# An order planner for attention and two gated layers on one core: measured lengths, a smaller early margin, eight drawn orders

## The chip, the cores and the metric

The kernel runs on one core of one Trainium2 chip. The metric is the device time of one execution in microseconds; the median of several runs counts. A program on one core has no other core to wait for.

## What is computed

The reference, cut to what matters (2 batches, 8 heads, 768 positions, heads of 64; blocks of 32 keys, a window of 16):

```python
k_sum = k.reshape(B, H, nb, block, D).max(axis=3)
v_sum = v.reshape(B, H, nb, block, D).mean(axis=3)
scores_l = where(|i - j| < window, scale * q @ k.T, -1e9)      # near keys
scores_s = scale * q @ k_sum.T + log(block)                    # one key per block
a = softmax(concatenate([scores_l, scores_s]))
x = a @ concatenate([v, v_sum])                                # [1536, 512]
h = sigmoid(x @ w_gate) * (x @ w_val)                          # 512 -> 1536
y = h @ w_out                                                  # 1536 -> 512
h2 = maximum(maximum(y @ w1, y @ w2), y @ w3)                  # 512 -> 768
out = h2 @ w_out2                                              # 768 -> 512
```

## The kernel before

The work is written as tasks. A task has an engine, a length in microseconds that stands in the code, a due time, the tasks that it needs, and the buffers that it takes and uses. `Plan.order` (line 123) is a list scheduler: it keeps a clock for each engine, takes at each step the task that can start first on its engine (among those within a small slack the one with the earliest due time), and so writes one order. `Plan.latest` walks that order backwards and gives each task the latest start that would not move the end; `Plan.refined` makes an order, takes these starts as new due times, orders again (`REFINE` is 2, so three orders in all), and keeps the one with the earliest end. The kernel is then emitted in that order. On the chip every engine runs its own instructions strictly in it, and what a task needs from another engine is waited for by semaphores. So a wrong length or landing time in the planner does no harm to the result, but an engine then stands at an instruction whose input is not there while later ones could run.

Transfers into the chip are issued by SyncE (SP) in one queue. The planner lets a landing follow the place in the queue, each transfer taking its length times `SLOW`, and adds a margin `LATE` of 2.0 us behind every transfer that ends after `CALM`, 4 us.

The attention is cut into 16 units: batch, pair of heads (4), half of the sequence. A unit's steps are: block maxima of the keys (`kmax`, line 802, VectorE); block sums of the values on TensorE (`vsum`, line 809), evacuated (814), folded (`vfold`, 817) and copied out (829); scores on TensorE, near keys (`k` or `kx` with `q` or `qx`) and block keys `ks` (both line 901); row maxima with the mask on VectorE (908); exponentials on ScalarE (914); a reciprocal on VectorE (919, 920); scaling on ScalarE (928) or VectorE (923); transposes on TensorE (933), evacuated by ScalarE (939, tile `at`); the product with the values (`v` or `vx`, line 946); and its split into two fp32r parts (465, 468). A unit whose number is even uses `v`, an odd one `vx`; in the first batch an odd head pair uses `kx` and `vnx`. Every fp32 weight block arrives as `raw`, is put into fp32 form on VectorE (535, 540, 544, tile `c` or `cx`) and split into two parts `w` on ScalarE and VectorE (465, 468).

The gated layer's matmuls for the first batch (line 1044, `x` with `w`, three for each of four chunks of the contraction, so 12 for one accumulator) begin once four units of the first batch are transposed; four PSUM banks `m` hold their accumulators, and each is freed by a sigmoid on ScalarE (1061) or a product on VectorE (1068). Exponential and sigmoid need different activation tables, so each change between them is an `ACT_TABLE_LOAD`. While the attention's first units run, TensorE has little to do; there, up to `FIRST` + 5 us of the planner's clock, the planner puts filler matmuls on a zero tile `idle` (line 1781) into its gaps, to keep its clock up. They are instructions like all others and have to run before what stands behind them.

Numbers at the ends of tile names, as in `e_432`, count buffers in the order in which they are taken; the first four units of the first batch are `e_149/150`, `e_236/237`, `e_333/334` and `e_432/433` in the kernel before and `e_149/150`, `e_202/203`, `e_326/327` and `e_474/475` in the changed one.

Of the kernel before, what the change touches and what calls it, by code (L numbers as in the profile page):

```python
# [14 lines left out]
ALU = mybir.AluOpType  # L15
# [6 lines left out]
FIRST = 28.0  # L22
# [18 lines left out]
REFINE = 2  # L41
SECOND_ORDER = (1, 2, 0)
# [5 lines left out]
SLOW = 1.12  # L48
BANKS_H, BANKS_W, BANKS_T = 9, 10, 5
# [30 lines left out]
class Plan:  # L80
# [7 lines left out]
    CALM, LATE = 4.0, 2.0  # L88
# [34 lines left out]
    def order(self):  # L123
# [18 lines left out]
        def earliest(t):  # L142
            at = free[t.eng]
            for d in t.deps:
                more = t.pad if d.eng != t.eng else 0.0
                if d.dma and d.end > self.CALM:
                    more = max(more, self.LATE)
                at = max(at, d.end + self.lag(d, t) + more)
            for d in t.after:
                at = max(at, d.start)  # L150
            need = {}
            for b in t.new:
                k = need.get(b.tag, 0)
                need[b.tag] = k + 1
                used = taken.setdefault(b.tag, [])
                i = len(used) + k - b.n
                if i >= 0:
                    for d in used[i].users:
                        if d.end is None:
                            return None  # L160
                        at = max(at, d.end + (self.LATE if d.dma and d.end > self.CALM else 0.1 if d.eng != t.eng else 0.0))
            return at
# [4 lines left out]
        while len(out) < len(self.tasks):  # L167
            best = None
            for e in engs:
# [91 lines left out]

    def refined(self, times):
        best = None
        for i in range(times + 1):
            out = self.order()
            if out is None:
                break
            end = max(t.end for t in out)
            if best is None or end < best[0]:
                best = end, out, {t: t.idle for t in out}  # L270
            start = self.latest(out) if i < times else None
            for t in self.tasks:
                if start:
                    t.due = start[t]
                    t.start = t.end = None
                    t.idle = 0
        for t, n in best[2].items():
            t.idle = n
        return best[1]
# [3 lines left out]
def kernel(  # L283
# [232 lines left out]
    def convert():  # L516
# [40 lines left out]
        def split(src, view, t, dep, n=512):  # L557

            w = Buf(wp, [128, 2, 512], F32R, "w", NW)
            k4 = add("ACT", 0.52 if n == 512 else 0.31, t - 1.0, lambda: hi(w.t[:, 0, 0:n], view()), dep, [w], [src], [prev.get("4")])  # L560
# [230 lines left out]
    def make_sums(b, p, T):  # L791
# [40 lines left out]
        if b == 0:  # L832
            vq = Buf(ap_, [128, 2 * D], F32, "vr", 1)
            v1 = add("PE", 0.55, T - 7, vsum, [lr, built], [ps], [r])
            v1 = add("ACT", 0.26, T - 6, vkeep, [v1], [vq], [ps])
            v2 = add("PE", 0.24, T - 5, vfold, [v1], [], [vq, ps])
        else:
            lr.after.append(pvs[UPB - 1])
            vr = Buf(ap_, [128, 2 * D], F32, "vr", 1)
            v1 = add("DVE", 1.2, T - 8, vadd, [lr, built], [vr], [r])  # L840
            v2 = add("PE", 0.16, T - 5, vmean, [v1], [ps], [vr])
            v2.pad = PAD
        v3 = add("ACT", 0.2, T - 4.5, vcopy, [v2], [vs], [ps])
# [4 lines left out]
    def make_unit(u, i):  # L848
# [110 lines left out]
        if whole:  # L959
            s0 = after("S", add("PE", 0.8, T - 11, lambda: scores(0, 96), [lk, lq], ps + e + [nm, sm], [q, kt]))  # L960
            s1 = add("PE", 0.45, T - 11, lambda: scores(96, CW), [s0, kk], [], [q, ks] + ps)
            s0.rows, s1.rows = 0.5, 0.25
            attention.append(s0)
        else:
            f1 = add("DVE", 0.23, T - 11.5, fill, [kk, lk], [], [kt, ks])
            s1 = after("S", add("PE", 1.0, T - 11, lambda: scores(0, CW), [f1, lq], ps + e + [nm, sm], [q, kt]))
            s1.rows = 0.45
            s1.pad = PAD
            attention.append(f1)
        AT = []  # L970
        E = []
        for h in range(2):
            m1 = add("DVE", 0.62, T - 9 + h, lambda h=h: maxi(h), [s1, built], [], [ps[h], e[h], nm])
            E.append(add("ACT", 1.14, T - 8 + h, lambda h=h: expo(h), [m1], [], [e[h], nm, sm], tab="E"))
            attention.extend([m1, E[h]])
        joint = i >= JOINT
        for h in range(2):
            if h == 0 or not joint:
                i1 = add("DVE", 0.27, T - 6 + h, lambda h=h: inverse(sm.t if joint else sm.t[:, h]),
# [5 lines left out]
            t1 = after("AT", add("PE", 0.30 if b else 0.45, T - 4.5 + h, lambda h=h: turn(h), [n1, built], [pa[h], at[h]], [e[h]]))  # L985
# [7 lines left out]
        g1 = add(*("ACT", 0.12) if dma else ("DVE", 0.46), T - 5, lambda: vfill(dma), [kv], [], [vt, vs], [lv])  # L993
        g1.dma = 0.63 if dma else 0.0
        pvs[i] = w1 = after("PV", add("PE", 0.95, T, pv, AT + [g1, lv], [px], [vt] + at))
# [119 lines left out]
    def make_forms(y0, y1, done, end, early, kept):  # L1115
# [4 lines left out]
        def form(name, src, view, dep, t):  # L1120
            f = Buf(late_pool, [128, 2, 2, HALF], F32R, "f", 7) if early else Buf(xp, [128, 2, 2, HALF], F32R, "x", 8)
            a1 = after("f" if early else "x", add("ACT", 0.74, t, lambda: hi(f.t[:, 0], view()), dep, [f], [src]))
            a2 = add("DVE", 0.85, t + 0.5, lambda: lo(f.t[:, 1], view(), f.t[:, 0]), [a1], [], [src, f])
            kept[name] = f, a2

        def diff(x, y_, dep, t, uses):
            u = Buf(late_pool, [128, 2, HALF], F32, "u", 2)
            k = after("u", add("DVE", 0.85, t, lambda: nc.vector.tensor_tensor(out=u.t, in0=x(), in1=y_(), op=ALU.subtract),  # L1128
# [15 lines left out]
    def make_x0(end):  # L1144
# [6 lines left out]
        for k in range(2):  # L1151
            h = xt[0, 0, k]
            sums.append(add("DVE", 0.85, end, lambda k=k, h=h: nc.vector.tensor_tensor(
# [3 lines left out]
        def diff(o, p, q, dep, t):  # L1157
            return add("DVE", 0.85, t, lambda: nc.vector.tensor_tensor(out=y(*o)(), in0=y(*p)(), in1=y(*q)(), op=ALU.subtract),
                       dep, [], [xs[k] for k in {o[0], p[0], q[0]}])

        def form(name, u, dep, t, f=None):
# [3 lines left out]
            a2 = add("DVE", 0.85, t + 0.5, lambda: lo(f.t[:, 1], y(*u)(), f.t[:, 0]), [a1], [], [xs[u[0]], f])  # L1165
# [374 lines left out]
    def make_h2():  # L1540

        for b in range(1):
            for a in range(2):
                for f in range(NF3):
# [5 lines left out]
                    k2 = add("DVE", 0.85, t + 0.5, lambda h=h, view=view: lo(h.t[:, 1], view(), h.t[:, 0]), [k], [], [src, h])  # L1550
# [4 lines left out]
    def make_G():  # L1555
# [7 lines left out]
        def split(dst, view, src, dep, t, wide, new, tag):  # L1563
# [3 lines left out]
            return add("DVE", 0.85 if wide else 0.469, t + 0.5, lambda: lo(dst(1), view(), dst(0)), [a1], [], [src, new])  # L1567
# [274 lines left out]
```

## Time and profile before

| | |
|---|---|
| median of 3 runs | 530.24 us (529.23 to 530.86) |
| the profiled execution | 531.51 us |
| its span | 529.8 us |
| busy: TensorE, its weight loads | 518.6, 495.4 us |
| busy: VectorE, ScalarE, GpSimd | 465.8, 328.9, 4.5 us |
| TensorE matmuls on `idle` | 40 |
| moved by DMA | 90.32 MB, 170 GB/s over the span |

The profile gives for each engine when it was busy, and for idle time what ended it. A busy TensorE includes the filler matmuls. Busy times of a window are cut at its edges, and pipelined matmuls overlap, so a step's length is best taken from one start to the next. Landings of transfers are seen only where somebody waits for them.

### The profile page before, as it was taken

How to read it: one execution, taken by the hardware profiler on the slowest of the kernel's cores; microseconds unless marked ns; L12 is line 12 of the kernel's file. 1: busy time of each engine (PE TensorE's matmuls, PEld its weight loads, DVE VectorE, ACT ScalarE, POOL GpSimd, SP SyncE). 2: the span in 40 equal slices, each digit the busy share in tenths (PEclk: the TensorE clock that was granted, in tenths of full speed). 3: DMA queues.
4: the chain of work that ended last, by engine and by line, in shares of the span. 5: the costliest groups of instructions: out<-in, count | busy, mean ns of one | idle time of the engine just before them, and what ended most of it. 6: DMA issues, size and time to landing. Idle time of an engine off the chain costs nothing.

```text
span 529.8 us, 10387 instructions
## 1 busy us (share of the span) xinstructions
PE 518.6 (98%) x3837; PEld 495.4 (94%) x3837; DVE 465.8 (88%) x1096; ACT 328.9 (62%) x784; POOL 4.5 (1%) x22
## 2 busy tenths in 40 slices
PE   7998999999999999999999999999999999999997
PEld 4687999999999999999999999999999999998897
DVE  5899999999998999998259999999999987899811
ACT  5799987897777984766356377355445334365421
POOL 3000000000000000000000000000000000000000
PEclk9899999999999999999999999999999999999999
DMA  8999598889888842158742037211322322201112
GB/s 249 291 328 364 176 320 313 301 252 362 292 297 290 294 132 80 40 199 299 275 142 79 1 120 279 80 40 43 118 79 80 123 80 76 80 1 40 61 61 80
DMA packets 33874, 90.32 MB, mean 170 GB/s; under 512 B 4000, under 2 KB 11296, under 8 KB 33824
## 3 DMA queue, kind: packets, MB, share of 16 engines
q1 hardware_dynamic: 31712, 87.51, 48.6%
q10 hardware_dynamic: 2112, 2.16, 1.3%
q8 instruction: 30, 0.49, 0.4%
q14 instruction: 20, 0.16, 0.1%
HBM read 67.04 MB, written 22.02 MB: 168 GB/s over the span
## 4 chain that ended last, share of the span: by engine, by line
PE 66%; DVE 18%; ACT 9%; DMA 3%; issue 1%; SPq 1%; ACTq 0%
PE m L1217 11%; PE s L1217 11%; PE m L1329 8%; PE s L1329 7%; PE m L1044 7%; PE m L1701 5%; PE m L1086 4%; PE s L1505 3%; PE m L1505 3%; PE s L1641 3%; DVE f L468 2%; ACT e L914 2%; DVE w L468 2%; DVE u L1128 2%; PE m L1641 2%; ACT e L928 2%
## 5 line engine op out<-in xcount | busy, mean ns | idle before, releaser
L1044 PE MATMUL m<-x,w 128*128 128x384 f32 x384 | 72.0, 340 | 0.8 <-ACT t L1061 0.8
L1086 PE MATMUL m<-h,w 128*128 128x384 f32 x384 | 71.1, 338 | 0.0
L1044 PEld LDWEIGHTS m<-x,w 128*128 128x128 f32 x384 | 65.8, 188 | 2.2 <-ACT t L1061 1.4
L1086 PEld LDWEIGHTS m<-h,w 128*128 128x128 f32 x384 | 66.3, 188 | 0.5 <-issue 0.3
L1329 PE MATMUL m<-f,w 128*128 128x384 f32 x324 | 61.8, 336 | 0.3
L1329 PEld LDWEIGHTS m<-f,w 128*128 128x128 f32 x324 | 56.3, 188 | 1.5 <-ACT t L1344 0.8
L1217 PE MATMUL m<-x,w 128*128 128x384 f32 x294 | 56.4, 334 | 0.3 <-ACT m L1290 0.3
L1217 PE MATMUL s<-f,w 128*128 128x384 f32 x294 | 55.9, 334 | 0.0
L1217 PEld LDWEIGHTS m<-x,w 128*128 128x128 f32 x294 | 51.4, 188 | 0.7 <-ACT m L1290 0.7
L1217 PEld LDWEIGHTS s<-f,w 128*128 128x128 f32 x294 | 51.4, 188 | 0.0
L1329 PE MATMUL s<-f,w 128*128 128x384 f32 x252 | 47.7, 335 | 0.0
L1329 PEld LDWEIGHTS s<-f,w 128*128 128x128 f32 x252 | 43.9, 188 | 0.2 <-ACT t L1344 0.2
L914 ACT ACTIVATE e<-e,nm 128x120 f32<-128x120 f32 x96 | 36.6, 384 | 7.6 <-DVE nm L908 7.5
L465 ACT ACTIVATE w<-raw 128x512 fp32r<-128x512 f32 (+1 forms) x52 | 29.0, 583 | 10.7 <-DVE raw L722 9.2
L465 ACT ACTIVATE w<-c 128x512 fp32r<-128x512 f32 (+1 forms) x50 | 28.5, 569 | 10.1 <-PE m L1217 3.9
L540 DVE SCALAR_TENSOR_TENSOR c<-raw,c 128x512 int32<-128x512 int32 x50 | 34.1, 683 | 0.1
L544 DVE SCALAR_TENSOR_TENSOR c<-raw,c 128x512 int32<-128x512 int32 x50 | 33.8, 680 | 0.0
L468 DVE TENSOR_TENSOR w<-c,w 128x512 fp32r<-128x512 f32 (+1 forms) x50 | 30.7, 615 | 3.5 <-ACT w L465 3.5
L468 DVE TENSOR_TENSOR w<-raw,w 128x512 fp32r<-128x512 f32 (+1 forms) x52 | 32.0, 631 | 0.5 <-ACT w L465 0.3
L465 ACT ACTIVATE h<-t 128x384 fp32r<-128x384 f32 x46 | 23.1, 518 | 8.7 <-DVE t L1389 3.2
L468 DVE TENSOR_TENSOR h<-t,h 128x384 fp32r<-128x384 f32 x46 | 25.2, 551 | 1.3 <-ACT h L465 1.1
L928 ACT ACTIVATE e<-e,sm 128x120 f32<-128x120 f32 x72 | 22.5, 385 | 5.5 <-DVE sm L920 5.5
(223 smaller groups left out, 984.2 us busy)
## 6 DMA issues: line engine op xcount, KB each, us to landing
raw<-in_wts_dram SPq DMA_DIRECT2D x60, 512.0 KB, 5.1
kept_o<-w SPq DMA_DIRECT2D x8, 512.0 KB, 5.3
kept_g<-w SPq DMA_DIRECT2D x6, 512.0 KB, 5.1
kept_v<-w SPq DMA_DIRECT2D x6, 512.0 KB, 3.8
w<-kept_o SPq DMA_DIRECT2D x6, 512.0 KB, 5.7
w<-kept_g SPq DMA_DIRECT2D x6, 512.0 KB, 5.7
w<-kept_v SPq DMA_DIRECT2D x6, 512.0 KB
k<-in_kw_dram SPq DMA_DIRECT2D x8, 360.0 KB, 6.6
```

Of the source, the lines that this page charges most:

```text
L465: nc.scalar.activation(out=dst, in_=src, func=ACTF.Copy)
L468: nc.vector.tensor_tensor(out=dst, in0=src, in1=h.bitcast(F32), op=ALU.subtract)
L540: nc.vector.scalar_tensor_tensor(out=c.t, in0=half(r, 1), scalar=-0x40000000, in1=c.t, op0=ALU.bitwise_and, op1=ALU.bitwise_or)
L544: nc.vector.scalar_tensor_tensor(out=c.t, in0=half(r, 0), scalar=29, in1=c.t, op0=ALU.logical_shift_right, op1=ALU.bitwise_or)
L914: nc.scalar.activation(out=e[h].t[:, t], in_=e[h].t[:, t], func=ACTF.Exp, scale=-1.0, bias=nm.t[:, h, t:t + 1], accum_out=sm.t[:, h, t:t + 1])
L928: nc.scalar.activation(out=e[h].t[:, t], in_=e[h].t[:, t], func=ACTF.Copy, scale=sm.t[:, h, t:t + 1])
L1044: nc.tensor.matmul(ps.t, lhsT=w.t.rearrange("p s (k f) -> p s k f", k=KC)[:, wh, kc], rhs=src[kc // 2].t[:, xh, kc % 2], start=(kc == 0 an ...
L1086: nc.tensor.matmul(ps.t, lhsT=w.t.rearrange("p s (k f) -> p s k f", k=KC)[:, wh, dm], rhs=h.t[:, xh], start=(i == 0 and j == 0), stop=(i = ...
L1217: nc.tensor.matmul(ps.t, lhsT=w.t[:, wh, c:c + 128], rhs=x.t[:, xh, kc], start=new and n == 0, stop=n == 5, skip_group_check=True)
L1329: nc.tensor.matmul(ps.t, lhsT=w.t[:, wh, c:c + 128], rhs=x.t[:, xh, kc], start=new and n == 0, stop=n == 5, skip_group_check=True)
L1505: nc.tensor.matmul(ps.t, lhsT=w.t[:, wh, c + 128 * m:c + 128 * m + 128], rhs=part(xh), start=new and q == 0, stop=q == 5, skip_group_check ...
L1641: nc.tensor.matmul(ps.t, lhsT=part(xh)[:, 128 * t:128 * t + 128], rhs=w.t[:, wh, c:c + 256], start=new and n == 0, stop=n == 8, skip_group ...
```

## The change

The lengths of some twenty tasks are set to other values (VectorE's splits of two chunks from 0.85 to 0.869, a copy of block sums from 0.46 to 0.585, the scores of the first batch from 0.8 and 0.45 to 0.64 and 0.43, and so on). Behind a transfer that ends before `FIRST`, 28 us, the margin becomes `SOON`, 0.5 us, in place of 2.0; transfers issued before `FIRST` take their length times `SLOW0`, 1.28, in place of 1.12. `refined` goes on after its three orders: eight times it moves the due times of the best order so far by normally distributed draws (seed, spread) for tasks that start before 250 us, orders again, in six of the eight once more with due times worked out backwards, and keeps an order that ends earlier. `order` also gets a branch for a given sequence, `seq`, which no call passes.

```diff
+STEPS = ((1003, 1.0, 0), (1005, 0.4, 1), (1008, 0.4, 1), (1080, 0.4, 0), (1129, 1.0, 1), ...
+UNTIL = 250.0
+SLOW0 = 1.28
-    CALM, LATE = 4.0, 2.0
+    CALM, SOON, LATE = 4.0, 0.5, 2.0
...
-                if d.dma and d.end > self.CALM:
-                    more = max(more, self.LATE)
+                if d.dma and not seq and d.end > self.CALM:
+                    more = max(more, self.LATE if d.end > FIRST else self.SOON)
...
-                ring = max(ring, dge + 0.65) + (t.dur * SLOW if t.eng == "SP" else 0.2)
+                ring = max(ring, dge + 0.65) + (t.dur * (SLOW0 if at < FIRST else SLOW) if t.eng == "SP" else 0.2)
...
+        for seed, spread, back in STEPS:
+            draw = random.Random(seed)
+            due = []
+            for d, s in zip(best[1], best[2]):
+                g = draw.gauss(0, spread)
+                due.append(d + g if s < UNTIL else d)
+            found = self.tried(due)
+            if found and back:
+                found = self.tried(self.back(found))
+            if found and found[0] < best[0]:
+                best = found
...
-            s0 = after("S", add("PE", 0.8, T - 11, lambda: scores(0, 96), [lk, lq], ps + e + [nm, sm], [q, kt]))
-            s1 = add("PE", 0.45, T - 11, lambda: scores(96, CW), [s0, kk], [], [q, ks] + ps)
+            s0 = after("S", add("PE", 0.64, T - 11, lambda: scores(0, 96), [lk, lq], ps + e + [nm, sm], [q, kt]))
+            s1 = add("PE", 0.43, T - 11, lambda: scores(96, CW), [s0, kk], [], [q, ks] + ps)
```

The new order differs from the first instruction on. Three places follow; the matmuls other than the fillers are the same ones, and the fillers go from 40 to 48.

The first is SP's queue of transfers, in before from its start without the two parts of the first `vn`:

```order
L781 DMA kx<-in_kn_dram 128x800
L781 DMA q<-in_qt_dram 128x384
L528 DMA raw<-in_wts_dram 128x1024
L781 DMA vnx<-in_vn_dram 64x1024
L781 DMA vnx<-in_vn_dram 32x1024
L781 DMA k<-in_kn_dram 128x800
L781 DMA qx<-in_qt_dram 128x384
L781 DMA v<-in_vw_dram 64x768
L781 DMA v<-in_vw_dram 32x768
L781 DMA kx<-in_kn_dram 128x800
L781 DMA q<-in_qt_dram 128x384
L781 DMA vx<-in_vw_dram 64x768
```

And the same stretch in the changed kernel, from the first weight block on; ahead of it stand `q`, `k`, `kx`, `q` and `vn`:

```order
L555 DMA raw<-in_wts_dram 128x1024
L808 DMA k<-in_kn_dram 128x800
L808 DMA vnx<-in_vn_dram 64x1024
L808 DMA vnx<-in_vn_dram 32x1024
L808 DMA qx<-in_qt_dram 128x384
L808 DMA v<-in_vw_dram 64x768
L808 DMA v<-in_vw_dram 32x768
L555 DMA raw<-in_wts_dram 128x1024
L808 DMA kx<-in_kn_dram 128x800
L808 DMA v<-in_vw_dram 64x768
L808 DMA v<-in_vw_dram 32x768
L808 DMA vx<-in_vw_dram 64x768
```

The third `k` moved ahead of `vnx`; a second weight block and the `v` of unit 2 moved ahead of `vx`; the `q` of unit 3, which followed the second `kx`, now follows `vx`.

The second is TensorE around the first dense matmuls (`x,w`). Before:

```order
L946 MATMUL s<-at,v 64x64 x12
L809 MATMUL s<-vnx,avg 32x128 x8
L933 MATMUL m<-ident,e_432 120x128 x3
L933 MATMUL m<-ident,e_433 120x128 x3
L817 MATMUL s<-vr,fold 32x128
L1044 MATMUL m<-x,w 128x384 x12
L946 MATMUL s<-at,vx 64x64 x12
L901 MATMUL s<-kx,qx 64x96 x12
L901 MATMUL s<-ks,qx 64x24 x12
L1044 MATMUL m<-x,w 128x384 x15
```

After:

```order
L973 MATMUL s<-at,v 64x64 x12
L960 MATMUL m<-ident,e_474 120x128 x3
L960 MATMUL m<-ident,e_475 120x128 x3
L1071 MATMUL m<-x,w 128x384 x9
L836 MATMUL s<-vnx,avg 32x128 x8
L1071 MATMUL m<-x,w 128x384 x9
L844 MATMUL s<-vr,fold 32x128
L928 MATMUL s<-kx,qx 64x96 x12
L928 MATMUL s<-ks,qx 64x24 x12
L1071 MATMUL m<-x,w 128x384 x6
```

The last value sum and its fold moved behind the start of the dense matmuls. Further ahead, 20 fillers now stand in a row before the product of unit 1 (`at,vx`), which is followed by the scores of unit 3, and 12 before the scores of unit 4; in before the longest rows are 11 at the start and 8 twice.

The third is ScalarE at its first change to the sigmoid's table. Before (`e_696`, `e_697` are the sixth unit, `e_804` the seventh; `t<-m` is the sigmoid):

```order
L914 ACTIVATE e_697,sm<-e_697,nm 128x120 x3
L939 ACTIVATE at<-s 120x384 x2
L928 ACTIVATE e_696<-e_696,sm 128x120 x3
L465 ACTIVATE w<-c 128x512
L1061 ACT_TABLE_LOAD
L1061 ACTIVATE t<-m 128x384
L465 ACTIVATE x<-s 128x384
L1013 ACTIVATE x<-s 128x384
L939 ACTIVATE at<-s 120x384
L465 ACTIVATE w<-cx 128x512
L939 ACTIVATE at<-s 120x384
L914 ACT_TABLE_LOAD
```

After (`e_703` is the sixth unit, `e_800` and `e_801` the seventh):

```order
L955 ACTIVATE e_703<-e_703,sm 128x120 x3
L492 ACTIVATE w<-c 128x512
L492 ACTIVATE x<-s 128x384
L1040 ACTIVATE x<-s 128x384
L941 ACTIVATE e_800,sm<-e_800,nm 128x120 x3
L966 ACTIVATE at<-s 120x384 x2
L941 ACTIVATE e_801,sm<-e_801,nm 128x120 x3
L1088 ACT_TABLE_LOAD
L1088 ACTIVATE t<-m 128x384
L492 ACTIVATE w<-cx 128x512
```

The sixth unit's evacuations `at` stood behind the load and the sigmoid and now stand ahead of them, and so do both exponentials of the seventh unit, which had a load of their own.

## Rows read from the trace of the kernel before

**Rows 1.** The page, part 1: TensorE's busy time, share and instructions.

```profile
PE 518.6 (98%) x3837; PEld 495.4 (94%) x3837; DVE 465.8 (88%) x1096; ACT 328.9 (62%) x784; POOL 4.5 (1%) x22
```

**Rows 2.** Windows: length, busy us of PE, PEld, DVE, ACT, POOL; clock, DMA, GB/s.

```profile
0.00:30.47 30.47, 25.87 (x448) 17.25 (x448) 21.90 (x95) 21.55 (x84) 4.54 (x22) 0.94 0.93 279
30.47:63.22 32.75, 30.98 (x403) 28.61 (x402) 32.10 (x99) 31.41 (x93) 0.00 (x0) 1.00 0.89 309
63.22:529.80 466.58, 461.79 (x2991) 449.51 (x2987) 411.85 (x904) 275.94 (x610) 0.00 (x0) 1.00 0.45 154
```

**Rows 3.** Windows, line 1781 (the fillers) alone: length, PE's busy us, clock, DMA.

```profile
0.00:30.47 30.47, 9.74 (x40) 0.94 0.93 279
```

**Rows 4.** Waits of PE: who, for whom, us in total, times, longest.

```profile
PE s L933 <- ACT at L939: 1.8, 1, 1.8
...
PE m L1044 <- ACT t L1061: 0.8, 2, 0.5
...
PE m L1217 <- ACT m L1290: 0.3, 1, 0.3
```

**Rows 5.** The chain that ended last, in order of time: start, us, what.

```profile
4.99 7.74 DMA vnx<-in_vn_dram
...
28.84 0.57 PE s L809 x16
...
36.73 2.27 ACT e L914 x12
...
47.42 0.97 PE s L901 x48
...
53.29 0.65 PE s L933 x6
...
117.88 10.11 PE m L1044 x57
```

**Rows 6.** Windows up to `vnx`'s landing and behind it: columns as in rows 2.

```profile
0.00:12.73 12.73, 9.15 (x139) 5.88 (x139) 6.81 (x35) 7.04 (x28) 4.54 (x22) 1.00 0.79 244
12.73:22.00 9.27, 8.72 (x170) 5.88 (x171) 6.81 (x23) 6.37 (x26) 0.00 (x0) 0.82 1.05 288
```

**Rows 7.** The timeline of PE, 15 to 32 us: start, us, line, operation, count.

```profile
15.91 1.10 PE L901 MATMUL s<-k,qx 64*64 64x96 f32 x24
...
17.21 0.92 PE L946 MATMUL s<-at,v 120*64 120x64 f32 x24
18.06 0.55 PE L901 MATMUL s<-ks,qx 64*64 64x24 f32 x24
18.53 0.41 PE L817 MATMUL s<-vr,fold 128*32 128x128 f32 x2
18.87 0.87 PE L933 MATMUL m<-ident,e 128*120 128x128 f32 x6
19.67 0.73 PE L901 MATMUL s<-kx,q 64*64 64x96 f32 x24
...
25.66 1.47 PE L1781 MATMUL s<-idle 128*128 128x384 bf16 x8
...
30.47 1.83 PE L1044 MATMUL m<-x,w 128*128 128x384 f32 x9
```

**Rows 8.** The timeline of ScalarE, 22 to 44 us: start, us, line, operation, count.

```profile
22.43 0.28 ACT L814 ACTIVATE vr<-s 128x128 f32<-128x128 f32 x1
...
27.76 0.96 ACT L928 ACTIVATE e<-e,sm 128x120 f32<-128x120 f32 x3
...
31.23 0.87 ACT L939 ACTIVATE at<-m 120x384 f32<-120x384 f32 x2
...
41.29 1.28 ACT L1061 ACT_TABLE_LOAD   x1
...
42.97 0.48 ACT L465 ACTIVATE x<-s 128x384 fp32r<-128x384 f32 x1
...
43.71 0.51 ACT L939 ACTIVATE at<-s 120x384 f32<-120x384 f32 x1
```

More of the change, by code (lines that the diff above doesn't have):

```diff
@@ L121, in run, with order @@
             return at
-    def order(self):
+    def order(self, seq=None):
         engs = ("PE", "DVE", "ACT", "POOL", "SP")
@@ L144, in earliest @@
             for d in t.deps:
-                more = t.pad if d.eng != t.eng else 0.0
-                if d.dma and d.end > self.CALM:
-                    more = max(more, self.LATE)
+                more = t.pad if d.eng != t.eng and not seq else 0.0
+                if d.dma and not seq and d.end > self.CALM:
+                    more = max(more, self.LATE if d.end > FIRST else self.SOON)
                 at = max(at, d.end + self.lag(d, t) + more)
@@ L160, in earliest @@
                             return None
-                        at = max(at, d.end + (self.LATE if d.dma and d.end > self.CALM else 0.1 if d.eng != t.eng else 0.0))
+                        at = max(at, d.end + ((self.LATE if d.end > FIRST else self.SOON) if d.dma and d.end > self.CALM and not seq else 0.1 if d.eng != t.eng else 0.0))
             return at
@@ L168, in order @@
             best = None
-            for e in engs:
+            if seq:
+                t = seq[len(out)]
+                best = earliest(t), t
+            for e in engs if not seq else ():
                 c = [(at, t) for at, t in ((earliest(t), t) for t in ready[e]) if at is not None]
@@ L260, in latest, with tried, back @@
         return start
+    def tried(self, due, seq=None):
+        for t, d in zip(self.tasks, due):
+            t.due = d
+            t.start = t.end = None
+            t.idle = 0
+        out = self.order(seq)
+        return out and (max(t.end for t in out), due, [t.start for t in self.tasks], out, [t.idle for t in self.tasks])
+    def back(self, found):
+        start = self.latest(found[3])
+        return [start[t] for t in self.tasks]
     def refined(self, times):
-        best = None
+        best, due = None, [t.due for t in self.tasks]
         for i in range(times + 1):
-            out = self.order()
-            if out is None:
+            found = self.tried(due)
+            if not found:
                 break
[L268 to L277, printed above, removed]
+            if best is None or found[0] < best[0]:
+                best = found
+            if i < times:
+                due = self.back(found)
+        for seed, spread, back in STEPS:
[4 more added lines that the diff above has]
+                due.append(d + g if s < UNTIL else d)
+            found = self.tried(due)
+            if found and back:
+                found = self.tried(self.back(found))
+            if found and found[0] < best[0]:
+                best = found
+        for t, n in zip(self.tasks, best[4]):
             t.idle = n
-        return best[1]
+        self.best = best
+        return best[3]
 @with_exitstack
@@ L965, in make_unit @@
             f1 = add("DVE", 0.23, T - 11.5, fill, [kk, lk], [], [kt, ks])
-            s1 = after("S", add("PE", 1.0, T - 11, lambda: scores(0, CW), [f1, lq], ps + e + [nm, sm], [q, kt]))
+            s1 = after("S", add("PE", 0.87, T - 11, lambda: scores(0, CW), [f1, lq], ps + e + [nm, sm], [q, kt]))
             s1.rows = 0.45
@@ L1127, in diff @@
             u = Buf(late_pool, [128, 2, HALF], F32, "u", 2)
-            k = after("u", add("DVE", 0.85, t, lambda: nc.vector.tensor_tensor(out=u.t, in0=x(), in1=y_(), op=ALU.subtract),
+            k = after("u", add("DVE", 0.869, t, lambda: nc.vector.tensor_tensor(out=u.t, in0=x(), in1=y_(), op=ALU.subtract),
                                dep + attention, [u], uses))
@@ L1152, in make_x0 @@
             h = xt[0, 0, k]
-            sums.append(add("DVE", 0.85, end, lambda k=k, h=h: nc.vector.tensor_tensor(
+            sums.append(add("DVE", 0.869, end, lambda k=k, h=h: nc.vector.tensor_tensor(
                 out=y(k, 0)(), in0=h.t[:, 0].bitcast(F32), in1=h.t[:, 1].bitcast(F32), op=ALU.add),
@@ L1566, in split @@
                 after(tag, a1)
[L1567 removed]
+            return add("DVE", 0.869 if wide else 0.469, t + 0.5, lambda: lo(dst(1), view(), dst(0)), [a1], [], [src, new])
         def form_h(f):
```

30 lines of the change are left out of this document (16 added, 14 removed).

## The prediction

> **What bounds the kernel now.** I read the page's busy shares first: TensorE (PE) is busy for 98% of the span [rows 1], so no other engine can be the bound over the whole run, and the time can change only by what PE does that is not work, or by when it waits. So I cut the span where the dense matmuls of the gated layer begin and where the last product of the first batch's attention ends (30.47 and 63.22 us) [rows 2]. Before 30.47 PE is idle for 30.47 - 25.87 = 4.60 us, and 9.74 us of what is called busy are the 40 filler matmuls on `idle` [rows 3]: that stretch holds only some 16 us of work. From 30.47 to 63.22 it is idle for 1.77 us, one wait, of the transposes of the sixth unit for a ScalarE evacuation [rows 4]. Behind 63.22 it is idle for 466.58 - 461.79 = 4.79 us, of which the list of waits names 0.8 + 0.3 = 1.1 us [rows 2, 4]; the rest is nearly all the tail after the last matmul, which the change does not touch. So all that an order can still give back is: a dense phase that starts earlier, 1.77 us, and 1.1 us.
>
> The number of real matmuls is the same in both orders. With X for the start of the dense phase and W for PE's waits behind it, the change of the time is then (X - 30.47) + (work moved from before X to behind it) + (W - 1.77) + what changes behind the first batch.
>
> **The edits.** New lengths, the early margin, `SLOW0` and the draws move instructions and cost nothing by themselves: the planner runs before the kernel does. The `seq` branch of `order` is passed by no call and does nothing. What is left is the order itself.
>
> **Term 1, the start X.** In the transfer queue of after, one more weight block stands ahead of the second `kx`, and the third `k` ahead of `vnx`, so small tiles land later; the two score operands `k`, `kx` of the first two units come first. How much later follows from bytes. By the shapes, the queue of before up to and with `vnx` holds 2464 KB (2.52 MB); `vnx` landed at 12.73 [rows 5], when at 244 GB/s [rows 6] 12.73 x 0.244 = 3.11 MB had moved. A transfer thus lands when the bytes moved are 0.58 MB past its place. From there to 22.0 the DMA engines are full (1.05 of their time, 288 GB/s [rows 6]), so I take the same rates for after. Then `vnx` (2864 KB, 2.93 MB) lands at 12.73 + (2.93 + 0.58 - 3.11) / 0.288 = 14.15, `qx` (3056 KB) at 14.8, the `vx` of unit 1 (4832 KB) at 21.1, and the query `q` of unit 3 (5024 KB) at 21.8; in before this `q` stood at 3936 KB, so 18.0.
>
> The PE queue of after is in order, so I walk it with the durations of before, each from one start to the next [rows 7] or from the chain [rows 5]: the value sums behind `vnx` 14.15 + 0.57 = 14.7; scores of unit 2 at 14.8 with their one filler (15.91 to 17.21) 1.30 = 16.1, their block part 0.47 = 16.6; products of unit 0 0.85 = 17.4; the fold 0.34 = 17.8; two sets of transposes 0.80 = 18.6; then 20 fillers at 1.47 / 8 = 0.18, 3.7 us = 22.3; products of unit 1 0.85 = 23.1 (their `vx` is there at 21.1); scores of unit 3 0.97 = 24.1 (its `q` at 21.8); one set of transposes 0.4 and the sums 0.57 = 25.1. ScalarE takes over with the sums' evacuation 0.28, the two exponentials of unit 3, 2.27 [rows 5], a short and a long evacuation 0.28 + 0.43, and the scaling 0.96 [rows 8] = 29.3; two sets of transposes 0.80 give **X = 30.1**. The slow scores row is in it (1.10 us for what takes 0.73 at 19.67 [rows 7], the granted clock being 0.82 over that stretch [rows 6]), since PE has gaps ahead of `vnx` in the new order as well. Bounds: nothing slow there and `vnx` half a microsecond earlier, 29.2; `vx` or `q` 3.5 us late, of which the walk has room for 1.1, 32.5. Term 1 is -0.37, from -1.3 to +2.0.
>
> **Term 2, moved work.** Both orders have five sets of scores, four units' transposes and three units' products ahead of X; after has one value sum (0.57) and one fold (0.34) behind it instead of before [rows 5, 7]: +0.91. In the other direction, nothing.
>
> **Term 3, the wait of 1.77 us.** In before, the first table load for the sigmoid (41.29, 1.28 us), the sigmoid and two copies stood on ScalarE ahead of the evacuation at 43.71 for which PE waited [rows 8]. In after, both evacuations of that pair stand ahead of the load, so this wait goes: -1.77. What is late next is the sigmoid itself, which frees the first of four accumulators. It was done at 42.97 [rows 8]; after puts two copies (42.97 to 43.71, 0.74), two exponentials (2.27) and two evacuations (0.87) ahead of it [rows 5, 8], 42.97 + 3.9 = 46.9. PE needs that accumulator after 48 matmuls at 10.11 / 57 = 0.177 (8.5), three units' scores (3 x 0.97), three units' products (3 x 0.85), four sets of transposes (2 x 0.65) and the moved 0.9 [rows 5, 7], at 30.1 + 16.2 = 46.3. So **W = 0.6**, from 0 to the 1.77 of before: +0.6.
>
> From the start of the table load (41.29) to the start of what follows the sigmoid (42.97) pass 1.68 us, 1.28 of them the load [rows 8]. The Trainium skill (ScalarE: Activation LUTs, "What ACT_TABLE_LOAD costs") adds about 1.38 us of drain to every switch, 2.66 in all; by that the sigmoid would come 1.4 later and the time would be 531.0. The trace does not agree: behind the load there is room for the sigmoid's 0.4 and for no drain, and the sum goes by the row; the drain has no chance of its own here.
>
> **Term 4, behind the first batch.** From 63.22 on the list of waits names 1.1 us. Longer VectorE lengths in the planner make its plan there more careful, while other orders can open new gaps: from -1.1 to +1.5, taken at 0. VectorE is the reason not to hope for more: between 30.47 and 63.22 it is busy for 32.10 of 32.75 us [rows 2], so a faster PE runs into it.
>
> **The sum.** -0.37 + 0.91 - 1.77 + 0.6 = -0.63 us. The profiled execution took 531.51 (span 529.8 and 1.7 around it), so 530.88; it lies 1.27 above the median of the runs, and from the median 530.24 the forecast is **529.6**. That is no change by the bound of 0.3% (1.6 us), about what a measurement of this kernel can tell.
>
> **The rivals.**
> *PE never waits (faster).* If ScalarE is ahead by more than I think, W is 0 and the named 1.1 us behind go too: -0.37 + 0.91 - 1.77 - 1.1 = -2.3, so 527.9. For it: the new order saves ScalarE one switch to the sigmoid and back before the last unit's exponentials, 2 x 1.28 us. Against it: VectorE at 98%, and a start that is set by landings.
> *Transfers land late (slower).* The smaller early margin lets the order count on `vx` and `q` of unit 3 soon after their place in the queue. The fillers end at 22.3, so the first 1.1 us of lateness are free; beyond that each microsecond moves X by one, since PE, VectorE's maxima and ScalarE's exponentials of unit 3 stand in a row. With 3.5 us, about what this `q` is moved back by already, X is 32.5 and the time 529.6 + 2.4 = 532.0; it decides from about 3.3 us. For it: engines at 1.05, a big block put ahead. Against it: the lag of 0.58 MB is measured in that very stretch.
> The Trainium skill (DMA: Bandwidth & Descriptors, "Latency and other measured facts") gives HBM's access latency as 0.2 us on average and 2 us at high load, which speaks against a margin of 0.5 us. With 1.8 us more than the walk has, X would be 30.8 and the time 530.3. No row here shows one transfer's latency apart from its queueing.
> *The order changes and the time does not.* The front is laid out anew, but the landings give the same X plus moved work, and the wait comes back at another place: -0.37 + 0.91 - 0.5 = about 0, so 530.2.
>
> **How the numbers follow.** The forecast has 0.48 (529.6, own range 528.7 to 531.2), no effect 0.10, the faster rival 0.25, late transfers or an equally large new wait behind the first batch 0.17. Faster by over 0.3% is the faster rival, 0.25, and 0.02 of the forecast's lower bounds; slower is the 0.17 and 0.01 of its upper bounds; within is 0.55. The range runs from somewhat below the faster rival's 527.9 (0.4, for X at its lower part) to the late transfers' 532.0: 527.5 to 532.0.
>
> **What would show it.** In the profile after: first dense matmul near 30.1; scores of unit 3 starting near 23.1 behind 20 fillers that PE does not wait after; no wait of transposes for a ScalarE evacuation near 44; a wait of some 0.6 us for the sigmoid's output near 46; PE's idle time behind the first batch near 4.8. The prediction is wrong if X lies below 29 or above 32, or if waits of more than 1.5 us appear between the dense start and 160 us.

## The result, and the profile after

The changed kernel is **slower**, by 0.6%: 533.71 us in the median of 11 runs (530.01 to 535.73) against 530.06 of 11 runs of the kernel before (529.23 to 531.31); the ratio is 1.0058, 95% interval 1.0035 to 1.0081. The forecast was 529.6 with a range to 532.0.

The page's busy line of the profiled execution answers to [rows 1]: TensorE has 8 matmuls more, all of them fillers.

```profile
PE 520.0 (98%) x3845; PEld 495.5 (94%) x3845; DVE 466.3 (88%) x1096; ACT 331.4 (63%) x786; POOL 4.5 (1%) x22
```

That execution took 530.01 us and is the shortest of the 11, so its trace alone shows no loss. The profiled execution of before (531.51) was in turn longer than nearly all others of its kernel. I therefore had the trace of a second execution of before, 530.09, and of three more of after. All of them, with X for the start of the dense matmuls as in the prediction:

| kernel, execution | time | granted clock, mean | X | from X to the end |
|---|---|---|---|---|
| before, the one of the rows | 531.51 | 0.996 | 30.47 | 499.33 |
| before, second | 530.09 | 1.000 | 29.11 | 499.19 |
| after, profiled with the result | 530.01 | 1.000 | 28.46 | 499.84 |
| after, second | 531.47 | 0.993 | 29.66 | 500.14 |
| after, third | 531.10 | 0.996 | 29.45 | 499.95 |
| after, fourth | 533.36 | 0.994 | 31.55 | 500.05 |

The second of before and the fourth of after are near the medians, and they are the pair to compare. Their difference is 533.36 - 530.09 = 3.27 us: 31.55 - 29.11 = 2.44 in the front and 500.05 - 499.19 = 0.86 behind it. The rest is nearly rigid: placed instruction by instruction on the execution of 530.01, the fourth is late by 3.12 us at the products of unit 1 (20.34) and by 3.09 at 513 us. So these two differ by what happened in their first 20 us. The one execution of after at full clock (530.01) is level with the second of before (530.09): its X is 0.65 us earlier and its rest 0.65 longer.

The windows answer to [rows 2], with the same columns (length, busy us of PE, PEld, DVE, ACT, POOL with counts, granted clock, DMA share, GB/s), cut at X. Before, second execution:

```profile
0.00:29.11 29.11, 23.45 (x449) 15.88 (x449) 21.86 (x95) 21.75 (x84) 4.54 (x22) 1.00 0.94 289
29.11:528.30 499.19, 492.78 (x3390) 478.14 (x3389) 443.83 (x1002) 307.32 (x702) 0.00 (x0) 1.00 0.48 164
```

After, fourth execution:

```profile
0.00:31.55 31.55, 27.26 (x438) 18.76 (x439) 22.34 (x90) 20.74 (x79) 4.54 (x22) 0.89 0.93 288
31.55:531.60 500.05, 494.98 (x3410) 478.50 (x3408) 443.97 (x1009) 310.84 (x708) 0.00 (x0) 1.00 0.48 162
```

Behind X, PE is idle for 5.07 us instead of 6.41, as an order with fewer waits should have it, and yet it is busy for 2.20 more. In the front the clock is 0.89 against 1.00. The front cut finer shows where, first before (second execution), then after (fourth):

```profile
7.00:13.20 6.20, 3.81 (x86) 2.46 (x76) 4.99 (x23) 6.11 (x28) 0.00 (x0) 1.00 0.98 311
13.20:20.10 6.90, 5.96 (x141) 4.33 (x143) 5.76 (x21) 4.86 (x20) 0.00 (x0) 1.00 1.03 301
```

```profile
7.00:13.20 6.20, 3.89 (x74) 2.32 (x74) 5.84 (x34) 5.33 (x27) 0.00 (x0) 0.98 1.03 314
13.20:20.10 6.90, 6.34 (x97) 5.06 (x98) 5.05 (x22) 5.15 (x20) 0.00 (x0) 0.52 1.02 310
20.10:31.50 11.40, 11.40 (x207) 8.08 (x206) 9.92 (x33) 8.93 (x33) 0.00 (x0) 1.00 0.94 301
```

From 13.2 to 20.1 us nearly all of after's stretch ran at the lower of the two levels, 1.2 GHz, and at 20.1 the clock was back at 2.4 GHz. What that does is read from the timeline of PE (start, us, engine, line, operation, count, idle time before it and what ended it). The fourth execution:

```profile
13.23 1.08 PE L836 MATMUL s<-vnx,avg 96*32 96x128 f32 x16 [0.88 <-DMA vnx<-in_vn_dram]
14.84 1.24 PE L928 MATMUL s<-k,qx 64*64 64x96 f32 x24 [0.53 <-PE s L836]
15.83 0.83 PE L928 MATMUL s<-ks,qx 64*64 64x24 f32 x24
16.59 0.50 PE L1808 MATMUL s<-idle 128*128 128x384 bf16 x1
17.02 1.55 PE L973 MATMUL s<-at,v 120*64 120x64 f32 x24
18.50 0.64 PE L844 MATMUL s<-vr,fold 128*32 128x128 f32 x2
19.07 1.21 PE L960 MATMUL m<-ident,e 128*120 128x128 f32 x6
20.12 3.41 PE L1808 MATMUL s<-idle 128*128 128x384 bf16 x20
23.46 0.92 PE L973 MATMUL s<-at,vx 120*64 120x64 f32 x24
```

The execution of 530.01, same instructions:

```profile
12.88 0.64 PE L836 MATMUL s<-vnx,avg 96*32 96x128 f32 x16 [0.53 <-DMA vnx<-in_vn_dram]
13.46 0.73 PE L928 MATMUL s<-k,qx 64*64 64x96 f32 x24
14.00 0.49 PE L928 MATMUL s<-ks,qx 64*64 64x24 f32 x24
14.43 0.34 PE L1808 MATMUL s<-idle 128*128 128x384 bf16 x1
15.10 0.92 PE L973 MATMUL s<-at,v 120*64 120x64 f32 x24 [0.33 <-ACT e L955]
15.95 0.41 PE L844 MATMUL s<-vr,fold 128*32 128x128 f32 x2
16.29 0.87 PE L960 MATMUL m<-ident,e 128*120 128x128 f32 x6
16.99 3.41 PE L1808 MATMUL s<-idle 128*128 128x384 bf16 x20
20.34 0.92 PE L973 MATMUL s<-at,vx 120*64 120x64 f32 x24
```

The two differ by 0.35 us at the value sums, by 1.38 at the scores behind them (14.84 against 13.46) and by 3.13 at the 20 fillers. The 1.38 are a late transfer. The profile puts the wait of 0.53 down to the value sums, but these had ended at 14.31; the scores need the query `qx` as well, and its transfer tells (what, issues, KB, us from issue to landing; the fourth first):

```profile
qx<-in_qt_dram SPq DMA_DIRECT2D x1, 192.0 KB, 8.1
qx<-in_qt_dram SPq DMA_DIRECT2D x1, 192.0 KB, 6.7
```

Issued at 6.67 and 6.60 us, it landed at 14.8 in the fourth execution and at 13.3 in the shorter one. So the value sums at half speed cost nothing there, since the scores had to stand until `qx` was there. The other 1.75 us are the low clock: from the scores to the fillers pass 5.28 us instead of 3.53, all of it work at about half speed, and a wait of 0.33 that only the shorter execution has is in the 3.53. From the fillers on, both run alike: 11.43 and 11.47 us to X.

Where the clock is low matters as much as for how long. In the second execution of after it is low for nearly all of the stretch from 7 to 13.2 us (windows as above):

```profile
7.00:13.20 6.20, 5.19 (x73) 3.77 (x74) 5.79 (x33) 4.99 (x25) 0.00 (x0) 0.53 1.04 308
```

Its X is 29.66, only 1.20 us behind that of the full clock: the slow steps lie in a stretch where the fourth execution has gaps.

### The profile page after: what moved, and what is told of

Same layout as the page of the kernel before. It is cut to its first block, busy times and chain, and to the rows that moved or that the text cites. A ratio compares the mean times of both kernels' runs of the same rounds, so it can differ in the third digit from the quotient of the medians.

```text
span 528.3 us, 10371 instructions
## 1 busy us (share of the span) xinstructions
PE 520.0 (98%) x3845; PEld 495.5 (94%) x3845; DVE 466.3 (88%) x1096; ACT 331.4 (63%) x786; POOL 4.5 (1%) x22
## 4 chain that ended last, share of the span: by engine, by line
PE 85%; ACT 8%; DVE 2%; DMA 2%; issue 1%; ACTq 1%; SPq 0%
PE s L1244 12%; PE m L1244 12%; PE m L1113 12%; PE m L1356 11%; PE s L1356 8%; PE m L1071 8%; PE m L1728 5%; PE s L1532 3%; PE m L1532 3%; PE s L1668 3%; ACT e L941 2%; PE s L973 2%; PE m L1668 2%; PE s L928 1%; DMA raw<-in_wts_dram 1%
## 5 line engine op out<-in xcount | busy, mean ns | idle before, releaser
L1071 PE MATMUL m<-x,w 128*128 128x384 f32 x384 | 74.2, 342 | 0.7 <-ACT t L1088 0.6
L1113 PE MATMUL m<-h,w 128*128 128x384 f32 x384 | 72.6, 338 | 0.4 <-ACT t L1088 0.4
L1244 PE MATMUL m<-x,w 128*128 128x384 f32 x294 | 56.4, 335 | 0.0
L1728 PE MATMUL m<-w,f 128*128 128x512 f32 x108 | 25.1, 390 | 0.0
```

The lines of the kernel that those rows point to most:

```text
L1071: nc.tensor.matmul(ps.t, lhsT=w.t.rearrange("p s (k f) -> p s k f", k=KC)[:, wh, kc], rhs=src[kc // 2].t[:, xh, kc % 2], start=(kc == 0 an ...
L1113: nc.tensor.matmul(ps.t, lhsT=w.t.rearrange("p s (k f) -> p s k f", k=KC)[:, wh, dm], rhs=h.t[:, xh], start=(i == 0 and j == 0), stop=(i = ...
L1244: nc.tensor.matmul(ps.t, lhsT=w.t[:, wh, c:c + 128], rhs=x.t[:, xh, kc], start=new and n == 0, stop=n == 5, skip_group_check=True)
L1728: nc.tensor.matmul(ps.t[:, c0:c1], lhsT=h.t[:, xh, e, c:c + 128], rhs=w.t[:, wh, c0:c1], start=(f == 0 and i == 0), stop=(f == NF2 - 1 and ...
```

## The experiments

Two theories stood after the result. The *clock theory*: the new order puts few fillers between 8 and 15 us, PE has gaps there, the granted clock falls in most executions, and what follows runs at half speed. The *rival*: transfers land late, as the prediction's slower case had it. Fillers were set by hand on the n-th task of PE, in after or before; everything else stayed as the planner made it:

```
+FILLERS = {4: 10, 5: 5, 7: 4, 8: 8, 11: 3}
-        for t in plan.refined(REFINE):
+        steps = plan.refined(REFINE)
+        on_pe = [t for t in steps if t.eng == "PE"]
+        for n, count in FILLERS.items():
+            on_pe[n].idle = count
+        for t in steps:
```

**The changed kernel again**, without an edit.

> The changed kernel as it is, for a trace of another execution: the first one traced had a mean granted clock of 1.000 and took 530.0 us, while the other ten had 0.987 to 0.996 and 531.0 to 535.7. Clock theory: the granted clock of TensorE drops to its lower level in the front (8 to 30 us) in most executions, and what stands there, the 20 and the 12 fillers above all, takes twice as long; the trace shows fillers of 0.3 us in the place of 0.16, the first dense matmul 1 to 5 us later than 28.5, and little new waiting on transfers; median 533 to 534. Rival, late transfers: waits of TensorE for vn, vnx, q or vx of 1 us and more each, and the low clock only follows from them.

Measured: 533.12 (531.47 to 533.98, 6 runs), ratio 1.0058 (1.0043 to 1.0072), granted clock 0.990 to 0.996 in all six. The loss comes again, and the full clock of the first trace was the exception. The trace (531.47) has marks of both theories: a wait of 1.87 us for `q`, as the rival named, and scores at the low clock behind it (1.24 us for what takes 0.73).

```profile
8.01 1.24 PE L928 MATMUL s<-kx,q 64*64 64x96 f32 x24 [1.87 <-DMA q<-in_qt_dram]
```

The 20 and the 12 fillers, which the clock theory expected to be slow above all, ran at full clock in it (3.41 and 2.00 us), as in every trace of after.

**More early fillers in after**, the edit above. The profile's page counts 3872 matmuls, so it is 27 more and not the 28 of the text.

> The changed kernel with 28 more fillers in TensorE's gaps between 8 and 15 us: 10 short ones ahead of the first value sums, 3 more ahead of the first transposes, 4 ahead of the second, 8 short ones ahead of vnx's sums, 2 more ahead of the first products. Clock theory: mean granted clock at least 0.998 in nearly all executions, times within 1 us of each other, median 529.5 to 530.5. Late transfers: the fillers change nothing about landings, so 533 to 534 as before them, with the same spread.

Measured: 531.1 (530.33 to 533.61, 11 runs), ratio 1.0020 (1.0007 to 1.0033); granted clock 0.999 or more in 10 of the 11, where after has that in 1 of 11. This is the test of the clock theory, since only work that computes nothing was added: about 2.0 to 2.6 us of the 2.9 to 3.7 that after lost in its two comparisons come back. The waits for transfers did not go with it: for `q` PE waits 0.78 and 1.38 us in the two traces of the filled order, 0.29 to 1.87 in the four of after. So late transfers by themselves do not explain this. But the median missed the 529.5 to 530.5 that the theory expected, and over 1 us stays: at full clock this kernel's median is 531.1 and that of the kernel before (19 of 27 executions beside it) 529.8.

**The 20 fillers taken out of after**: `FILLERS = {15: 0}`.

> The changed kernel without its row of 20 fillers ahead of the second unit's products. Clock theory: at the lower clock these 20 take about 6.4 us instead of 3.3, so without them the slow executions lose 2 to 3 us, but TensorE stands idle in their place and the clock can drop there instead: 531 to 533. Late transfers: the row only fills a wait, so no change, 533 to 534.

Measured: 533.32 (530.69 to 535.45, 10 runs), ratio 1.0057 (1.0038 to 1.0076). The 20 fillers are not what costs: the clock theory expected 531 to 533 here, and the value lies where the rival had put it. In the traced execution (532.53) the sums of `vnx` start at 14.62 after a wait of 1.94, the clock is low in both early windows, and it is not wholly back in the third, where the other traces show 1.00:

```profile
7.00:13.20 6.20, 4.79 (x74) 3.27 (x74) 5.76 (x33) 5.18 (x26) 0.00 (x0) 0.72 1.05 310
13.20:20.10 6.90, 5.48 (x93) 4.25 (x94) 4.69 (x21) 4.74 (x19) 0.00 (x0) 0.61 1.02 299
20.10:31.50 11.40, 9.92 (x195) 7.66 (x194) 11.14 (x42) 10.14 (x37) 0.00 (x0) 0.93 0.94 302
```

**Eight early fillers taken out of before**: `FILLERS = {2: 0, 3: 0}`.

> The kernel before without 8 of its early fillers (6 short ones ahead of the first value sums and 2 ahead of the second unit's scores). Clock theory: those kept the clock up there, so the mean granted clock falls below 0.996, the spread grows and the median rises to 531 to 533. Late transfers: nothing to do with fillers, 530.0 to 530.3 as before.

Measured: 530.88 (529.40 to 531.81, 11 runs), ratio 1.0017 (1.0006 to 1.0027); clock 0.992 to 0.997 in ten of the eleven. The clock does what the theory says, but the price is 0.64 us by the medians and 0.9 by the ratio, a fifth to a third of what after loses and less than the 531 to 533 expected. So a lower clock in the front does not cost a fixed amount, as the second execution of after showed already; it costs what the steps behind it cannot take up.

**One edit undone at a time**, first the draws, `STEPS = ()`.

> The changed kernel without its eight drawn orders (STEPS = ()); lengths and margins stay new. Its order has 12 fillers ahead of the first scores, then 2 and 2 up to the products of unit 0, then 11 and 5, then 25 short ones of 128 columns; the gated layer's first matmuls stand in 21 pieces up to the end of the first batch instead of 26. Clock theory (TensorE's granted clock falls in the front when few fillers stand between 8 and 15 us): as few early fillers as in the changed kernel, so a granted clock near 0.993 again, and 533.1 less 5 cuts at 0.1 = 532.6. Rival, the draws themselves are what costs (an order drawn to end early in the plan ends late on the chip): without them 530.2 to 530.5, at whatever clock.

Measured: 532.36 (530.34 to 532.84, 6 runs), ratio 1.0037 (1.0022 to 1.0052), clock 0.990 to 0.997. The median is near the 532.6 of the clock theory, but its trace (532.84) loses at other places. The front is at full clock in spite of a wait of PE of 2.7 us for `v` of the first products, and X is still 30.34. The rest takes 500.66, with a wait of 2.3 for a sigmoid's output, and there, behind X, the clock falls: the 12 dense matmuls behind the wait took 3.80 us, where 12 take 2.36 to 2.38 at full clock in the other traces.

```profile
55.68 3.80 PE L1071 MATMUL m<-x,w 128*128 128x384 f32 x12 [2.25 <-ACT t L1088]
```

The early margin, `SLOW0 = 1.12` and `SOON = 2.0`.

> The changed kernel with the old early margin alone (SLOW0 = 1.12, SOON = 2.0); lengths and draws stay new. Its order has 11 fillers, then 5, then 18 of 128 columns, then 3, 9 and 11 ahead of the dense matmuls, which stand in 23 pieces instead of 26. Clock theory: the early gaps are filled again, granted clock 0.999, and the kernel before plus two or three cuts at 0.1, so 530.2 to 530.8. Rival, the draws or the lengths cost and not the margin: near 533 as the changed kernel.

Measured: 532.13 (531.58 to 532.98, 5 runs), ratio 1.0041 (1.0028 to 1.0053), clock 0.997 to 1.000. The clock was foretold, the time was not: this order is near full clock and still 2 us over before. Of the three edits undone, only this one holds the clock at 0.997 or more in all its executions. Its windows show another loss, a front that ends late at full clock, with the same work in it and 91 fillers instead of 40:

```profile
0.00:32.63 32.63, 27.81 (x499) 19.66 (x500) 25.43 (x101) 23.26 (x88) 4.54 (x22) 1.00 0.91 277
32.63:530.50 497.87, 492.80 (x3392) 478.17 (x3390) 441.52 (x995) 300.64 (x693) 0.00 (x0) 1.00 0.48 163
```

The task lengths, back at their old values.

> The changed kernel with the old task lengths; margin and draws stay new. Its order has 12 fillers, then 1 and 2 up to the products of unit 0, 10 of 128 columns, 1, 12 and 2; the dense matmuls stand in 26 pieces as in the changed kernel. Clock theory: few early fillers, granted clock near 0.993, 533. Rival, the lengths cost (a plan with longer steps is laid out worse): 530.2 to 530.8.

Measured: 531.92 (530.60 to 533.67, 6 runs), ratio 1.0043 (1.0029 to 1.0057), clock 0.990 to 0.999. Both expectations miss, 533 and 530.2 to 530.8. In its trace (530.60) X is 27.59, the earliest of all, and the rest takes 501.3, the longest of after and its variants.

So no one of the three edits is the culprit: without any one of them 1.8 to 2.2 us of loss stay. That each gives something back is likely by the medians and not shown, since the intervals of the three ratios (1.0022 to 1.0057) overlap with those of after (1.0035 to 1.0081). Each variant lays out another order, and its one trace loses at another place, in the front or behind it. I could not tell from these runs which edit matters most for the time.

**Cuts in dense runs.** Behind X, PE is busier in after without more work than 0.92. The dense matmuls up to the end of the attention stand in 41 runs instead of 38, and more of them are short (14 of at most six matmuls instead of 8). To price a cut by itself, fillers of 64 columns went into 24 places of before:

```
+CUTS = 24
...
+        cuts = [t for o, p, t in zip(on_pe, on_pe[1:], on_pe[2:]) if t.new and o.dur == p.dur == t.dur == 0.52][:CUTS]
...
+            if t in cuts:
+                nc.tensor.matmul(t.new[0].t[:, 0:64], lhsT=idle[:, 0:128], rhs=idle[:, 0:64], start=True, stop=True)
```

> The kernel before with one extra filler of 64 columns put ahead of 24 accumulations that stand inside long runs of dense matmuls, into the accumulator that the next matmul clears. Work added is 24 x some 0.03 us (a filler of 384 columns takes 0.17 at full clock). If a cut in a run of dense matmuls costs nothing by itself, the time rises by 0.7 us, to 530.9. If each cut costs about 0.1 us besides, as the pieces of three matmuls between transposes suggest (0.61 from one start to the next instead of 0.53), it rises by 24 x 0.13 = 3.1, to 533.3, and the trace shows each piece later by 0.13 than the one ahead of it.

Measured: 532.68 (531.05 to 533.77, 7 runs), ratio 1.0043 (1.0027 to 1.0060). Both expectations miss, the real value lies between them. In the trace, the stretch from X to the first matmul on `w,f` takes 448.60 us instead of 446.42 and 446.49 in the two of before: 2.1 us, 0.09 for each cut, the filler's own 0.04 included. The timeline shows it:

```profile
68.20 0.20 PE L1787 MATMUL m<-idle 128*128 128x64 bf16 x1
68.24 2.33 PE L1045 MATMUL m<-x,w 128*128 128x384 f32 x12
70.42 0.20 PE L1787 MATMUL m<-idle 128*128 128x64 bf16 x1
```

From one filler to the next pass 2.22 us for 12 matmuls, which take 12 x 0.177 = 2.12 within the long run of [rows 5]. By the starts of the single matmuls in the traces, the first step after a cut or a wait takes 0.26 to 0.28 us, nearly every other one 0.17 to 0.18.

**Single executions**, for the traces of the table above.

> The changed kernel once more, one look, to have the trace of an execution near its median of 533.4 (the two traced so far took 530.01 and 531.47). If the loss of its ordinary executions lies in the front, the dense matmuls start at (time - 1.7 - 500.0): at 28.3 for 530.0, 31.7 for 533.4, with the granted clock low between 7 and 16 us, and from there to the end pass 499.8 to 500.3 us. Rival, the loss lies behind the front (waits for sigmoid outputs, cuts): the dense start stays at 28.5 to 29.7 and the rest grows to 502 or more.

> The same again, for a second such trace. Front theory: dense start at (time - 1.7 - 500.0), rest 499.8 to 500.3. Rival: dense start 28.5 to 29.7, rest 502 or more.

> The kernel before once more, one look: its first traced execution took 531.51 at a granted clock of 0.996, most others near 530 at 1.0. Front theory: at 530.0 the dense matmuls start near 29.0 instead of 30.47, with no slow rows from 12.7 to 22 us, and from there to the end pass 499.3 us again. Rival: dense start 30.4 as before, and the rest 497.9.

Measured: 531.10, 533.36 and 530.09; X at 29.45, 31.55 and 29.11; from X to the end 499.95, 500.05 and 499.19. The front theory holds in each, and the rival (a longer rest) in none. One detail missed: the low clock was expected between 7 and 16 us, and in the execution of 533.36 it lay between 13.2 and 20.1.

**The filled order again.**

> The changed kernel with 28 more early fillers once more, one look: its first trace had 501.02 us from the dense start to the end, 0.9 more than the changed kernel's 499.84 to 500.14, in waits for sigmoid outputs (1.0, 0.4, 0.3). If these belong to the order, they come again and the rest is 501; if they were chance, the rest is 500.0, so the front is what a filled order can mend and 0.7 us over the 499.33 of the kernel before remain for cuts and moved work.

Measured: 530.48, X at 28.63, rest 500.07. The 0.9 us in the first trace of this order (rest 501.02) did not come back. Its front ran at full clock throughout, PE being busy for 5.60 us from 7 to 13.2 instead of 3.89, in spite of a wait of 1.38 us for `q`:

```profile
7.00:13.20 6.20, 5.60 (x103) 4.08 (x104) 5.83 (x34) 5.44 (x27) 0.00 (x0) 1.00 1.03 335
13.20:20.10 6.90, 6.90 (x118) 4.87 (x118) 6.64 (x25) 6.78 (x27) 0.00 (x0) 1.00 1.04 320
```

No version here beats the kernel before.

## Why the prediction was wrong

**Where it was right.** The wait of 1.77 us [rows 4] is gone. The sigmoid's output is late next, as term 3 said: W was forecast at 0.6 near 46 us, and the waits of after behind X (who, for whom, total, times, longest) begin with it, 0.36 at 46.43 and 0.27 at 58.67:

```profile
PE m L1071 <- ACT t L1088: 0.6, 2, 0.4
PE m L1113 <- ACT t L1088: 0.4, 1, 0.4
PE m L1356 <- ACT t L1371: 0.3, 1, 0.3
```

In the second execution of before there stand instead:

```profile
PE s L933 <- ACT at L939: 1.7, 1, 1.7
PE m L1044 <- ACT t L1061: 0.8, 2, 0.5
PE m L1217 <- ACT m L1290: 0.3, 1, 0.3
```

Term 2's moved work, forecast at 0.91, is 0.58 + 0.34 = 0.92 by its matmuls' starts. Behind the first batch, PE's idle time is 4.07 us in the first trace of after and 4.31 in the fourth, not the 4.8 that stood for no change; term 4's gain is real and small. And in the execution of 530.01 the new table load has the sigmoid right behind it, 1.30 us after its start:

```profile
44.59 1.28 ACT L1088 ACT_TABLE_LOAD   x1
45.89 0.49 ACT L1088 ACTIVATE t<-m 128x384 f32<-128x384 f32 x1
```

The Trainium skill (ScalarE: Activation LUTs, "What ACT_TABLE_LOAD costs") would have a drain of 1.38 us besides; the trace does not agree with it here either.

**The step that failed is term 1.** It was -0.37 and is +2.44 between the two ordinary executions. It failed twice. Of the 3.9 us between the forecast change (-0.63) and the measured one (+3.27), 1.36 are the base, 1.45 the walk, and 1.1 the rest behind X.

*The base.* X of before was taken as 30.47, from an execution that the prediction itself put 1.27 us above the median, and the gain was then subtracted from the median. But those 1.27 us lie in the very term that was being forecast: the second execution of before has X at 29.11 and the same rest to 0.14 us. Against 29.11 the forecast's own X of 30.1 is +1.0, and with the other terms as they stood the sum would have been -0.63 + 1.36 = +0.7, or 530.9 and still "no change". The hint stood in [rows 6]: a granted clock of 0.82 behind 12.73, which I carried into the walk as one slow row and did not ask whether the other executions had it.

*The walk.* It gave the new order's steps behind `vnx` the durations of [rows 5] and [rows 7], most of them at full clock. In the fourth execution they took a third to three quarters longer: products of unit 0 1.48 instead of 0.85, the fold 0.57 instead of 0.34, transposes 1.05 instead of 0.80, scores and their block part 1.75 with no filler in it where the walk had 1.77 with one. The scores started where the walk had them, at 14.84 for 14.8, with `qx` landed just ahead of them. The 20 fillers then started at 20.12, not at 18.6, and X came at 31.55 instead of 30.1. In the full-clock execution the same walk is 1.6 us too long, since there `qx` landed at 13.3 and no row was slow. So the order fixes X only within 3 us. The bounds for X, 29.2 to 32.5, hold three of the four executions, and of the signs of being wrong (X below 29 or above 32) only the full-clock execution gave one, by 28.46; against the right base the same bounds would have stood for +0.1 to +3.4 instead of -1.3 to +2.0.

**Term 4 left out the seams.** The rest grew by 0.51 to 0.95 us where terms 2 to 4 gave -0.26. The named waits fell from 2.8 to 1.3 us where term 3 gave 1.17 less, the moved work is as forecast, and about 1.3 us of busy time came on top (2.20 more busy, 0.92 of it moved work). The seams are part of it: by the starts of single matmuls, 52 steps between dense matmuls take 0.25 to 0.3 us instead of 46, at 0.1 each 0.6 us. The other 0.7 are spread thinly: there are 41 instead of 38 steps from a dense matmul to other work, but without the waits they take 0.22 us on average in both. What the cut pieces cost besides the experiment's 0.09 for each is argued from the trace, not shown by a run of its own.

**The rivals.** Slower was priced at 532.0 and had 0.17; its sign was right, its mechanism as it was written wrong. PE did not wait after the 20 fillers, for `vx` or for `q` of unit 3, in any trace of after. Late landings have a share all the same, ahead of the 20 fillers: `qx` landed at 13.3, 14.3, 13.2 and 14.8 in the four executions, and in the fourth it set the scores back by 1.38 us against the first. The small margin seems to matter by another road too: an order that counts on early landings puts its fillers elsewhere, and where a landing then lets PE wait, PE idles. That the old margin brought the clock back speaks for it; the chain itself is argued. In the fourth execution four such gaps lie between 6.8 and 13.2 us (0.63, 0.54, 0.53 and 0.88), none of them long.

**What stays open.** When the clock falls is not settled. In the windows from 7 to 13.2 us PE is busy for 3.89 us in the fourth execution of after, where it fell, and for 3.81 in the second of before, where it did not. More fillers raise the odds of a full clock from 1 in 11 to 10 in 11; no trace here tells the outcome of one execution beforehand. A long wait alone does not decide it either: 1.87 us for `q` came with a low clock in the second execution of after, 2.7 us for `v` without one in the variant without draws. How much of the loss over all executions late landings carry is open, and so is why the filled order stays over 1 us above before. Nor is it shown which of the edits made the rest busier.

## What to carry to other kernels

Where a few executions disagree by more than the effect that is sought, find the stretch in which they differ before taking durations from any of them, and do not take a term from one execution and the base from the median. Work that computes nothing may still be bought and paid for: an order that has its filler matmuls elsewhere than in the gaps that really open can lose the clock of the work behind them. This planner does keep a clock of its own (`Plan.Clock`), but it prices the gaps of the plan, and the plan's gaps follow from its landing times. When the place of small work among dense matmuls changes, count the cuts and price them from a trace, as one counts waits.

## What the runs showed of the hardware

At the same program the granted clock of one stretch of 7 us was 0.52 in one execution and 1.00 in another. The times differ by 3.35 us, of which 1.75 arose in the slow steps and 1.38 in a transfer that landed later. Fillers of 384 columns took 0.17 us each right behind the slow stretch: the row of 20 took 3.41 us both in the execution whose clock had been 0.52 until then and in that with 1.00, so the clock was back at its higher level by their start.

Behind the front, executions of one order repeat very closely: from X to the first matmul on `w,f` four executions of after and the filled order's second took 446.98 to 447.00 us, and two of before 446.42 and 446.49. The exception is the first of the filled order, 447.94, 0.4 us of it in waits for sigmoid outputs that its second did not have.
